# A single-core attention and MLP kernel, with and without TensorE's waits on its own finished work

## The chip, the core and the metric

The kernel runs on one core of a Trainium2 chip. A core has a matrix engine (TensorE, in the profile PE for its matmuls and PEld for its weight loads), a vector engine (VectorE, DVE), a scalar engine (ScalarE, ACT), a general engine (GpSimd, POOL) and a sync engine (SyncE, SP), which here only issues transfers. Each engine works through an instruction list of its own, and the lists meet only at semaphores: an instruction may wait until a semaphore has reached a count, and may raise one when it is done. The metric is the time of one execution on the device in microseconds (us).

## The reference

The computation has two parts, both in bfloat16. Part A is an attention layer with a memory that is carried from segment to segment. The 2048 tokens (512 wide) are normalised and cut into 64 segments of 32. For each segment, 8 memory rows are put ahead of the 32 tokens, and 32 heads of width 128 attend over the 40 rows. The first 8 rows of the output become the next segment's memory, so the 64 segments form a chain. Part B is an MLP (512 to 1792 to 512, with gelu) behind two layer norms.

```python
for s in range(n_seg):
    h = jnp.concatenate([mem, x[:, s*32:(s+1)*32, :]], axis=1)
    q, k, v = (jnp.einsum('btd,dhe->bhte', h, W) for W in (Wq, Wk, Wv))
    scores = jnp.where(mask, jnp.einsum('bhqe,bhke->bhqk', q, k) * scale, -1e9)
    o = jnp.einsum('bhqk,bhke->bhqe', _softmax(scores), v)
    o = jnp.einsum('bhte,hed->btd', o, Wo)
    mem = o[:, :8, :]
    outs.append(o[:, 8:, :])
h = x + concatenate(outs)
h2 = h + MLP(layernorm(layernorm(h)))
```

## The kernel before

Every operation is first recorded as an `Op` in a planner (`Sched`), with what it reads and writes and an expected duration. For TensorE one `Op` is a unit: a short fixed group of weight loads and matmuls, such as the four weight loads and four matmuls that make one 128-row step of a projection (`passes`, lines 931 to 952; its matmuls have line 946, its weight loads 944 and 946, and the matmuls that keep the weights of the unit before have line 689). Other units are the scores of the critical 8 rows (SC, line 1122), the full scores (SA, line 1179), the products with V (PV0, PV1 and PVA, lines 1153, 1157, 1225 and 1231) and the output projection (WO, line 1264, 8 units of 16 instructions; wo_B at line 1303 for a block of four segments).

The order of the units on TensorE is written out by hand (`ORDERS`): for each segment Q, K, V, the critical scores, filler work of the next block (F), the products, WO, SA. For the other engines `schedule` places each operation by planned times. `wire` then turns the dependencies into semaphore waits. Within TensorE no waits are needed, since its units run in order; `wire` gives it waits on ACT, DVE, POOL and on transfers alone.

Three further steps treat TensorE's instruction list as pieces of 256 instructions (`FETCH_N`), counted from `FETCH_AT`:

- `pads` (from line 497) adds up to 8 weight loads to a unit, which repeat a load that could have been left out. These shift where the borders between pieces fall. It chooses them by a cost over the planned time between two borders and over a lateness that depends on the unit in which the border falls (`LATE`).
- `windows` (from line 395) gives SyncE's transfers planned times between the borders.
- `pauses` (from line 374) looks at every unit that is the first to start behind a border (`heads`, set in `align`). Among the units that start within the next `PAUSE_IN` = 64 instructions, it takes the first `PAUSES` = 3 that wait for nothing, and makes each wait until TensorE's own last unit that was planned to end `PAUSE_US` = 0.5 us before it has ended. That earlier unit then raises TensorE's semaphore if it did not do so already.

`pauses` is the last step of `finalize`, behind the second `wire`. `emit` calls `align` once more behind it; there a unit's length in instructions counts half of its waits rounded down, so one wait adds nothing. The instruction list holds 156 heads, and `pauses` adds 407 waits: 116 in WO units, 147 in Q and K units, 71 in V units, 52 in F units and 21 outside the segments. It adds 156 semaphore increments, which makes 1266 on TensorE in all.

Of the kernel before, what the change touches and what calls it, by code (L numbers as in the profile page):

```python
# [27 lines left out]
LATE = dict(Q0=0.1, K0=0.1, Q1=-0.5, K1=-0.4, V0=2.0, SC0=2.0, SC1=1.6, V1=1.8, F=1.3, PV0=1.0, PVA=1.0, PV1=0.95, WO=0.4, F2=0.5, SA=0.5)  # L28
KEEP = True
WINDOWS, WIN_LO, WIN_HI, WIN_BEHIND = True, 1.0, -0.8, 0.4  # L30
PAUSES, PAUSE_IN, PAUSE_US = 3, 64, 0.5
KEPT, LEAD = 3, 9
REST = (0, 1, 4, 5, 6, 8, 9)
ORDER0 = (6, 7, 8, 9, 10, 11, 0, 1, 2, 3, 4, 5, 12, 13)
# [1746 lines left out]
```

## Time and profile before

| | |
|---|---|
| median of 3 runs | 804.04 us (802.3 to 804.13) |
| the profiled execution, whole | 805.6 us |
| its span, first to last instruction | 803.9 us |
| mean granted TensorE clock | 0.996 |
| TensorE matmuls busy | 770.4 us (96%) |
| VectorE, ScalarE, GpSimd busy | 73%, 66%, 39% |

The span holds an opening of some 52 us in which weights arrive, 63 segments of about 10.3 us up to about 700 us, and the MLP. The profile names each group of instructions by source line, engine, operation and the tiles it writes and reads, gives the idle time of the engine ahead of it, and what ended that idle time. "issue" as the ender means that the profile shows nothing that the engine waited for. Idle times under 0.15 us are not listed.

### The profile page before, as it was taken

The page shows a single profiled execution, that of the slowest core. Times are in us where ns is not written, and L with a number is a line of the kernel's source. Part 1 is how long each engine was busy: PE and PEld are TensorE (multiplying, and loading weights), DVE is VectorE, ACT ScalarE, POOL GpSimd, SP SyncE. Part 2 cuts the span into 40 slices and gives each one's busy share as a digit, 9 for nine tenths or more (in the row PEclk, how much of TensorE's full clock was granted, in tenths as well). Part 3 has the DMA queues.
Part 4 walks back from the last instruction along what each step waited for, and adds up shares of the span by engine and source line. Part 5 has one row for each costly group of instructions (what it writes and reads, how often), then busy time and mean ns, then how long its engine had stood idle before and what let it go on. Part 6 is the DMA issues. An engine that isn't in the chain of part 4 may idle for free.

```text
span 803.9 us, 44855 instructions
## 1 busy us (share of the span) xinstructions
PE 770.4 (96%) x19573; PEld 423.6 (53%) x20093; DVE 585.3 (73%) x1865; ACT 529.2 (66%) x1381; POOL 311.4 (39%) x836
## 2 busy tenths in 40 slices
PE   4788999999999999999999999999999999999998
PEld 1345455555555555556665555556556564544443
DVE  3267888888888888888888888888888887833111
ACT  1446777767776777776767777777776777653342
POOL 3013223444343444444434444444453425276200
PEclk9989999999999999999999999999999999999999
DMA  8960000111201010103020201030112222266200
GB/s 337 393 194 11 3 21 20 24 38 23 37 15 46 10 50 10 44 11 57 4 52 8 52 9 50 11 50 4 50 31 62 45 58 53 62 184 157 53 27 26
DMA packets 65453, 48.11 MB, mean 60 GB/s; under 512 B 29028, under 2 KB 61676, under 8 KB 65260
## 3 DMA queue, kind: packets, MB, share of 16 engines
q1 hardware_dynamic: 64928, 44.98, 20.4%
q8 instruction: 156, 2.56, 1.4%
q14 instruction: 37, 0.30, 0.1%
q10 hardware_dynamic: 332, 0.27, 0.1%
HBM read 31.08 MB, written 8.13 MB: 49 GB/s over the span
## 4 chain that ended last, share of the span: by engine, by line
PE 91%; DMA 2%; DVE 2%; SPq 2%; issue 1%; ACT 1%; DVEq 0%
PE high L946 33%; PE high L689 17%; PE quad L1264 15%; PE quad L1667 6%; PE high L1660 5%; PE high L1303 3%; DMA WQ<-in_A_Wq_dram 2%; SPq L849 2%; PE quad L1122 2%; PE quad L1179 2%; PE quad L1225 2%; PE high L1459 2%; PE high L1153 1%; PE quad L1153 1%; PE high L1264 1%
## 5 line engine op out<-in xcount | busy, mean ns | idle before, releaser
L946 PE MATMUL high<-WQ,hT 128*32 128x512 bf16 x1796 | 158.2, 383 | 3.8 <-DVE hT L1270 3.0
L1202 POOL TENSOR_TENSOR PA<-SA,rsa 128x256 bf16<-128x256 f32 x64 | 39.6, 619 | 235.5 <-DVE rsa L1194 148.0
L689 PE MATMUL high<-WK,hT 128*32 128x512 bf16 x1260 | 127.3, 379 | 0.1
L1264 PE MATMUL quad<-WO,OT 128*32 128x256 bf16 x4032 | 122.7, 273 | 0.2 <-issue 0.2
L946 PE MATMUL high<-WV,hT 128*32 128x512 bf16 x1528 | 117.0, 381 | 0.0
L965 ACT ACTIVATE kq<-high 128x512 bf16<-128x512 f32 x160 | 94.2, 598 | 26.7 <-PE high L946 23.3
L964 ACT CAST kq<-high 128x512 bf16<-128x512 f32 x161 | 93.7, 582 | 21.4 <-PE high L946 19.6
L1264 PEld LDWEIGHTS quad<-WO,OT 128*32 128x32 bf16 x4032 | 101.9, 97 | 6.9 <-issue 1.7
L1210 POOL COPY BD<-PTA 32x128 f32<-32x128 f32 x256 | 79.6, 311 | 16.3 <-DVE PTA L1206 0.6
L946 PEld LDWEIGHTS high<-WQ,hT 128*32 128x32 bf16 x1796 | 52.8, 95 | 62.0 <-issue 28.9
L987 DVE STREAM_TRANSPOSE KALL<-kq 128x256 f32<-128x256 f32 x160 | 69.4, 434 | 10.9 <-ACT kq L964 8.1
L964 ACT CAST VS<-high 128x512 bf16<-128x512 f32 x126 | 73.1, 580 | 0.0
L944 PEld LDWEIGHTS <-hT 128*32 128x32 bf16 x3064 | 50.7, 96 | 32.7 <-DVE hT L1270 6.3
L1276 DVE STREAM_TRANSPOSE TT<-quad 128x256 f32<-128x256 f32 x63 | 28.3, 449 | 50.8 <-PE quad L1264 50.7
L1663 ACT ACTIVATE WQ<-high,b1t 128x512 bf16<-128x512 f32 x42 | 28.9, 687 | 51.9 <-PE high L1660 51.9
L964 ACT CAST OT<-quad 128x128 bf16<-128x128 f32 (+1 forms) x128 | 47.8, 375 | 21.8 <-PE quad L1157 21.5
L1021 ACT COPY KALL<-KALL 128x128 f32<-128x128 f32 x62 | 18.5, 298 | 59.0 <-PE quad L1179 58.8
L987 DVE STREAM_TRANSPOSE QT<-kq 128x256 f32<-128x256 f32 x128 | 54.8, 428 | 1.9 <-ACT kq L965 1.6
L946 PE MATMUL high<-WK,hT 128*32 128x512 bf16 x788 | 55.4, 379 | 0.0
L1122 PEld LDWEIGHTS quad<-KALL,ZC 128*32 128x32 bf16 x2016 | 32.3, 96 | 42.2 <-POOL BD L1210 18.1
L689 PE MATMUL high<-WV,hT 128*32 128x512 bf16 x520 | 54.5, 387 | 0.0
L1316 POOL TENSOR_TENSOR opT<-TTB,TTS 32x64 bf16<-32x64 f32 x128 | 40.0, 312 | 35.0 <-DVE opT L1270 18.6
(182 smaller groups left out, 1612.4 us busy)
## 6 DMA issues: line engine op xcount, KB each, us to landing
WV<-in_A_Wv_dram SPq DMA_DIRECT2D x4, 1024.0 KB, 10.5
WK<-in_A_Wk_dram SPq DMA_DIRECT2D x4, 1024.0 KB, 18.5
WQ<-in_A_Wq_dram SPq DMA_DIRECT2D x4, 1024.0 KB, 20.4
WO<-in_A_Wo_dram SPq DMA_DIRECT2D x16, 256.0 KB, 7.6
v_last<-VSB SPq DMA_DIRECT2D x60, 64.0 KB, 2.2
VBD<-v_last SPq DMA_DIRECT2D x60, 64.0 KB, 2.6
h_mid<-xr SPq DMA_DIRECT2D x16, 128.0 KB, 2.0
WQ<-h_mid SPq DMA_DIRECT2D x4, 512.0 KB, 4.2
```

Of the source, the lines that this page charges most:

```text
L689: return e.add_instruction(mybir.InstMatmult(name="I-%d" % (4000000 + _kept[0]), engine=mybir.EngineType.PE, start_tensor_calc=start, stop ...
L944: e.ldweights(l, tile_position=(0, 32 * j))
L946: ins = e.matmul(o, l, m, start=(k == 0), stop=(k == DC - 1), tile_position=(0, 32 * j), skip_group_check=True)
L964: return {"act": (lambda e: e.copy(out, src), t_act(n, ps_)), "dve": (lambda e: e.tensor_copy(out, src), 0.155 + 1.0e-3 * n * fast)}
L965: return {"act": (lambda e: e.mul(out, src, scale_), t_act(n, ps_)), "dve": (lambda e: e.tensor_scalar(out, src, scale_, None, ALU.mult), ...
L987: S.op("dve", lambda e: e.transpose(out, src), reads=[("kq", i)], writes=[key], dur=t_dve(256) + 0.02)
L1122: ins = e.matmul(o[32 * j:32 * j + 32, :], zc_window(h), rhs, start=False, stop=(i == 3), tile_position=(0, 32 * j), skip_group_check=True)
L1210: S.narrow(S.op("pool", lambda e, j=j, rows=rows: e.tensor_copy(words(BD[rows, par, :, j, :, :]), words(PTA[rows, 0:4])), reads=["PTA"], w ...
L1264: ins = e.matmul(ps[bank][32 * j:32 * j + 32, 0:256], lhs(slot(h)), wo_cols(h, b), start=(k == 0), stop=(k == 15), tile_position=(0, 32 * ...
L1316: return e.tensor_tensor(o[32 * q:32 * q + 32, c:c + 2], x, y, ALU.add)
L1660: ins = e.matmul(ps[bank][:, 0:SBT], W1[:, cc, fc * P:(fc + 1) * P], hnT_of(k)[:, cc, :], start=(cc == 0), stop=(cc == DC - 1))
L1667: S.op("pe", lambda e: e.matmul(quad[:, t, :], gT_of(k, fc)[:, t * P:(t + 1) * P], W2[:, fc, :], start=(fc == (0 if k else ORDER0[0])), st ...
```

## The change

One constant changes, and with it `pauses` adds no wait and no increment. The waits on other engines and on transfers stay.

```diff
-PAUSES, PAUSE_IN, PAUSE_US = 3, 64, 0.5
+PAUSES, PAUSE_IN, PAUSE_US = 0, 64, 0.5
```

The loop that reads it:

```python
for first in self.heads:
    n, i = 0, first
    while n < PAUSES and i < len(pe) and pe[i].at < pe[first].at + PAUSE_IN:
        o = pe[i]
        j = bisect.bisect_right(ends, o.start - PAUSE_US) - 1
        if not o.waits and 0 <= j < i:
            o.waits = [pe[j]]
            pe[j].sig = True
            n += 1
        i += 1
```

## The prediction

> **What bounds the kernel now.** I read the page first, its busy shares and its chain, and then asked the trace for the idle time of TensorE alone.
>
> ```profile
> span 803.9 us, 44855 instructions
> PE 770.4 (96%) x19573; PEld 423.6 (53%) x20093; DVE 585.3 (73%) x1865; ACT 529.2 (66%) x1381; POOL 311.4 (39%) x836
> PE 91%; DMA 2%; DVE 2%; SPq 2%; issue 1%; ACT 1%; DVEq 0%
> ```
>
> TensorE's matmuls (PE) are busy for 96% of the span and make 91% of the chain that ended last. The weight loads (PEld) run beside them at 53%. A change that only touches TensorE's stream can win what idle time that stream has, or add to it. The next view splits the span: each row gives the stretch, its length, and then the busy time of PE, PEld, DVE, ACT and POOL.
>
> ```profile
> 0.00:52.00 52.00, 31.98 (x481) 13.63 (x465) 17.05 (x41) 17.53 (x40) 7.07 (x30) 0.93 0.96 348
> 52.00:93.00 41.00, 36.59 (x1100) 21.21 (x1132) 31.52 (x104) 26.10 (x73) 13.46 (x38) 1.00 0.10 18
> 93.00:350.00 257.00, 255.00 (x7401) 145.07 (x7564) 217.11 (x708) 188.61 (x513) 107.22 (x299) 1.00 0.12 27
> 350.00:660.00 310.00, 308.16 (x8916) 178.15 (x9352) 262.89 (x860) 227.08 (x619) 133.81 (x369) 1.00 0.16 35
> 660.00:702.00 42.00, 39.89 (x1140) 21.64 (x1032) 33.89 (x108) 29.15 (x77) 17.00 (x46) 1.00 0.23 60
> 702.00:803.90 101.90, 98.79 (x564) 43.95 (x552) 22.89 (x48) 40.74 (x61) 32.88 (x54) 1.00 0.34 88
> ```
>
> The opening (20.0 us idle) waits for weights to arrive, which the change does not touch. In the steady middle, 93 to 660 us, PE is idle for 257.00 - 255.00 + 310.00 - 308.16 = 3.8 us. What is that idle time? The waits of the matmul stream from 70 to 660 us (total us, times, longest):
>
> ```profile
> PE quad L1179 <- issue: 2.1, 8, 0.4
> PE high L946 <- DVE hT L1270: 1.5, 2, 0.8
> PE high L946 <- issue: 0.7, 3, 0.4
> PE high L1153 <- DVE PTC L1139: 0.5, 1, 0.5
> PE high L1157 <- issue: 0.3, 2, 0.2
> PE quad L1264 <- issue: 0.2, 1, 0.2
> ```
>
> Fourteen of these sixteen waits (8 + 3 + 2 + 1) are "issue": TensorE waits for nothing that the profile can name. They sum to 2.1 + 0.7 + 0.3 + 0.2 = 3.3 us. Two of them in order of time:
>
> ```profile
> 307.96 0.21 PE L1179 MATMUL quad<-KALL,QT 128*32 128x40 bf16 x5
> 308.48 0.35 PE L1179 MATMUL quad<-KALL,QT 128*32 128x40 bf16 x27 [0.31 <-issue]
> ...
> 616.93 0.39 PE L946 MATMUL high<-WQ,hT 128*32 128x512 bf16 x3
> 617.67 0.39 PE L946 MATMUL high<-WQ,hT 128*32 128x512 bf16 x1 [0.35 <-issue]
> ```
>
> The break falls inside one group of equal matmuls: after 5 of the 32 of L1179, after 3 of the 4 of L946. No tile can be missing there, since the group's operands were complete before its first matmul. What is missing is the next instruction. The profile shows that instructions come in pieces:
>
> ```profile
> q8 instruction: 156, 2.56, 1.4%
> ```
>
> 2.56 MB in 156 transfers is 16.4 KB each, and 1.4% of 16 engines' 803.9 us over 156 is an estimated 1.15 us per transfer. Between 93 and 350 us there are 7401 + 7564 matmuls and weight loads, which is 58 pieces of 256 in 257 us, or 4.4 us a piece. So each piece has to be requested, brought (1.15 us) and taken up within about 4.4 us, and at 14 of the some 132 borders between 70 and 660 us (by the same 4.4 us, an estimate) it came late. [...]
>
> **The change, part by part.** With PAUSES at 0 the loop in `pauses` adds nothing. Walking the program's own instruction list, I count 156 heads (first unit behind a border), 407 waits of TensorE on its own semaphore, and 156 semaphore increments that exist for these alone (of 1266). All 407 waits and 156 increments go. Nothing moves: the order on every engine, the padding weight loads, the borders and the DMA windows are all fixed before or without these waits, and a single wait rides in the weight load that has it, so no instruction is saved.
>
> *The waits themselves, against the path.* A wait costs time if TensorE runs dry at it. The matmul rows above name no release by PE. The weight-load port does:
>
> ```profile
> PEld high L946 <- PE high L946: 9.5, 28, 0.5
> PEld L944 <- PE high L946: 3.0, 7, 0.7
> PEld L944 <- PE high L689: 0.4, 1, 0.4
> PEld quad L1264 <- PE high L1157: 0.2, 1, 0.2
> ```
>
> At 28 + 7 + 1 + 1 = 37 places an own-work wait was the last thing that a weight load waited for; the port stood idle 9.5 + 3.0 + 0.4 + 0.2 = 13.1 us before them, 0.35 us each. Matmuls already issued cover that idle time: PE shows no gap there. Direct gain: 0 at one end; at the other, all 3.8 us of idle time of the middle, if "issue" hid them. I take 0, because the breaks above fall inside groups, where no such wait stands (a wait stands at a unit's first instruction). If the cover were gone the waits would cost up to 13.1 us now, and removing them would win it; nothing in the rows says that it is gone.
>
> *The increments.* 156 increments fewer on matmuls that run anyway: 0, from both sides, since no engine but TensorE reads these values.
>
> *The side effect on the fetch.* The 407 waits all stand in the first 64 instructions behind a border, so right behind the point at which one piece is used up and the next has to be asked for. While the front of TensorE's stream is held, it cannot run on through the new piece. Whether a hold brings the request forward, or holds it up, no row shows; this is the unknown of the forecast. I bound it. Its size per place is the hold itself, 0.35 us. Its number lies between 0 and 37 places (holds that were the last release). So the slip of the fetch sums to between 0 and 37 x 0.35 = 13 us, in the one direction or the other. A slip costs only where the piece is already just in time. That share lies between 14 of 132 borders (0.1, those which stall now) and all. I take a quarter, nearer the low end because that is the end with a row. And I take the direction "later without the waits": the stream then runs on, with the units behind the border already to be sent, before the next stop gives room, and the next stop is another engine's wait or a full stream. Cost: 37 x 0.35 x 0.25 = 3.2 us, between 1.3 (a tenth) and 13.
>
> *Where a later fetch hits.* TensorE stalls a little more at L1179 and at the first units of L946, as now. Vector, Scalar and GpSimd then wait for PE and shift with it: DVE at 73% and ACT at 66% have room, so nothing else becomes late first.
>
> *Sum.* 0 (waits) + 0 (increments) + 3.2 (fetch) = +3.2 us. The profiled execution took 805.6 us for its span of 803.9; on that basis the changed kernel takes 808.8. The median of the runs shown is 804.04, 1.6 us below the profiled one, and the forecast is for such a median: 804.04 + 3.2 = 807.2 us.
>
> [...]
>
> **The rivals.**
>
> *Nothing happens.* The request is made when the border is crossed, whatever stands behind it. All 407 waits stand behind it, so none can delay or hasten it. For it: 370 of the 407 are not seen to be the last release of anything. Against it: the 37 that are. Time: 804.0 us. [...]
>
> *Faster.* The waits sit at the front of the stream just behind the border, and what is held there delays the taking up of the piece, so that the following border is reached with less in hand. Without them TensorE arrives with more work already issued and the 14 breaks shrink. Price: the breaks' 3.3 us, and as the profile counts PE as busy to the modelled end of a matmul (379 ns in the row below, against a start every 0.22 us in the timeline), some 0.16 us more at each: 3.3 + 14 x 0.16 = 5.5 us if all go, half of it if half do.
>
> ```profile
> L689 PE MATMUL high<-WK,hT 128*32 128x512 bf16 x1260 | 127.3, 379 | 0.1
> ...
> 616.71 0.40 PE L689 MATMUL high<-WK,hT 128*32 128x512 bf16 x4
> ```
>
> Half gives 801.3 us, all 798.5. It decides from half of the breaks on (2.8 us is over what can be told). Against it: the holds are covered and long over when the next border comes 4.4 us later.
>
> *Much slower.* Each of the 37 holds is what makes the request early, and every border is just in time: 13 us, 817 us. For it: TensorE has 3.8 us of idle time in 567, so a delay has nowhere to go. Against it: 118 of 132 borders show no stall, so most have some slack.
>
> *That the change does not do what it says* can only mean that waits of other kinds remain: of the units behind borders many wait for ACT, DVE or POOL anyway. Those hold the front too and weaken the effect; this belongs to "nothing happens".
>
> **How the numbers follow.** A measurement of this kernel can tell about 0.3%, 2.4 us: the runs shown lie between 802.3 and 804.13. Chances: a slower fetch as forecast, 0.50 (its own range 805 to 813); nothing, 0.32; faster, 0.12; much slower, 0.06. Slower by over 0.3% (above 806.5) needs 2.4 us: I give that 0.40 of the first case's 0.50, and the last case's 0.06, so 0.46. Within 0.3%: 0.32, 0.10 of the first and 0.03 of the faster case, 0.45. Faster: 0.09. The range goes from 801.5 (most of the faster case at half price) to 814 (short of the extreme).
>
> **What would show it.** Right: the "issue" rows of the matmul stream grow from 14 events and 3.3 us in 70 to 660 us to some 20 to 25 events and 5 to 6 us, with breaks inside groups; the middle's PE idle time grows from 3.8 to about 7 us; the weight-load rows released by PE vanish; the instruction queue still shows 156 transfers. If idle "issue" stays at 3.3 us and the time too, the waits had no hold on the fetch. If "issue" falls, the direction was wrong. The prediction fails outright if the loss appears at another place than at borders, such as in waits for DVE or ACT.

## The result, and the profile after

The changed kernel takes 822.75 us (median of four, 818.5 to 824.5) against 803.76 us of the kernel before (median of four with one execution more than ahead of the prediction, 802.3 to 804.13): a ratio of 1.0234, interval 1.0211 to 1.0258. It is slower, as forecast, but by 19 us where the forecast was 3.2 us and its range ended at 814 us.

The profiled execution of the changed kernel took 818.5 us and lies 4.2 us below its median; the one before took 805.6 us, 1.6 us above its median. The two traces therefore differ by 818.5 - 805.6 = 12.9 us, and the sums below are made against that. The page of the changed kernel, its span, busy shares, chain, instruction queue and its output projection (matmul count, busy time and mean ns, idle time ahead):

```profile
span 816.8 us, 44855 instructions
...
PE 771.5 (94%) x19573; PEld 423.3 (52%) x20093; DVE 586.1 (72%) x1865; ACT 529.7 (65%) x1381; POOL 310.9 (38%) x836
...
q8 instruction: 156, 2.56, 1.3%
...
PE 90%; issue 2%; DMA 2%; DVE 2%; SPq 2%; ACT 1%; DVEq 0%
...
L1264 PE MATMUL quad<-WO,OT 128*32 128x256 bf16 x4032 | 125.9, 273 | 13.1 <-issue 13.1
```

The L1264 row on the page of before:

```profile
L1264 PE MATMUL quad<-WO,OT 128*32 128x256 bf16 x4032 | 122.7, 273 | 0.2 <-issue 0.2
```

The same work is done in the same pieces: counts and transfers are those of before, and the order of the instructions is the same on every engine. What grew is "issue", and on one line: L1264, the output projection WO, now stands idle for 13.1 us where it stood for 0.2 us.

The stretches of the steady middle (columns as in the prediction), here 93 to 672 us since the segments end later:

```profile
93.00:358.00 265.00, 259.20 (x7496) 144.90 (x7644) 220.20 (x720) 191.82 (x522) 108.81 (x305) 1.00 0.11 26
358.00:672.00 314.00, 305.12 (x8803) 177.83 (x9268) 258.88 (x845) 223.01 (x609) 131.74 (x364) 1.00 0.15 34
```

PE is idle for 5.8 + 8.9 = 14.7 us of it, against 3.8 us before. The clock column says 1.00 in both, as before. The waits of the matmul stream from 70 to 672 us (total us, times, longest) say at what:

```profile
PE quad L1264 <- issue: 11.7, 16, 1.3
PE high L946 <- DVE hT L1270: 1.5, 2, 0.8
PE quad L1179 <- issue: 1.3, 4, 0.3
PE high L1153 <- DVE PTC L1139: 0.5, 1, 0.5
PE high L1303 <- issue: 0.4, 1, 0.4
PE high L1157 <- issue: 0.2, 1, 0.2
PE high L946 <- issue: 0.2, 1, 0.2
```

The two waits for VectorE are unchanged to the tenth. "Issue" went from 14 events and 3.3 us to 23 events and 11.7 + 1.3 + 0.4 + 0.2 + 0.2 = 13.8 us, and 16 of the 23 are at WO. One of them in the timeline:

```profile
453.79 0.50 PE L1264 MATMUL quad<-WO,OT 128*32 128x256 bf16 x9
455.11 1.71 PE L1264 MATMUL quad<-WO,OT 128*32 128x256 bf16 x55 [0.82 <-issue]
456.55 0.70 PE L1303 MATMUL high<-WO,OTB 128*32 128x512 bf16 x8
```

A group of 64 equal matmuls is broken after 9, and the other 55 come 0.82 us late. The reading is again that the next instruction piece is missing, and the place fits it: counted out in the program's own instruction list, in pieces of 256, the late matmul is the first, the second or the fourth instruction behind a border at all 14 "issue" stops of before and at all 23 of now.

Listed idle time grew by 13.8 - 3.3 = 10.5 us, and the profile counts the modelled end of each matmul as busy. What the stops cost is better seen by setting each unit's first matmul in one trace beside the same one in the other. Segments 5 to 60 take 14.6 us more than before, and 14.8 us more in their WO units alone; the other units come to -0.2 us. Segment 5, on the other hand, starts at 91.1 us and before at 92.9 us, so the trace of the changed kernel had a shorter opening. 14.6 - 1.8 = 12.8 us is the difference of the traces to within 0.1 us.

### The profile page after: what moved, and what is told of

The parts are those of the page before. It is cut to its first block, busy times and chain, and to the rows that moved or that the text cites. A ratio compares the mean times of both kernels' runs of the same rounds, so it can differ in the third digit from the quotient of the medians.

```text
span 816.8 us, 44855 instructions
## 1 busy us (share of the span) xinstructions
PE 771.5 (94%) x19573; PEld 423.3 (52%) x20093; DVE 586.1 (72%) x1865; ACT 529.7 (65%) x1381; POOL 310.9 (38%) x836
## 4 chain that ended last, share of the span: by engine, by line
PE 90%; issue 2%; DMA 2%; DVE 2%; SPq 2%; ACT 1%; DVEq 0%
PE high L946 32%; PE high L689 17%; PE quad L1264 15%; PE quad L1667 6%; PE high L1660 5%; PE high L1303 3%; DMA WQ<-in_A_Wq_dram 2%; PE quad L1179 2%; PE quad L1122 2%; SPq L849 2%; PE quad L1225 2%; PE high L1459 2%; PE high L1153 1%; PE quad L1153 1%; PE high L1264 1%
## 5 line engine op out<-in xcount | busy, mean ns | idle before, releaser
L946 PE MATMUL high<-WQ,hT 128*32 128x512 bf16 x1796 | 157.6, 380 | 3.4 <-DVE hT L1270 3.0
L1264 PE MATMUL quad<-WO,OT 128*32 128x256 bf16 x4032 | 125.9, 273 | 13.1 <-issue 13.1
L946 PE MATMUL high<-WV,hT 128*32 128x512 bf16 x1528 | 116.5, 380 | 0.0
L1264 PEld LDWEIGHTS quad<-WO,OT 128*32 128x32 bf16 x4032 | 102.0, 97 | 22.5 <-issue 17.9
L946 PEld LDWEIGHTS high<-WQ,hT 128*32 128x32 bf16 x1796 | 52.4, 95 | 61.1 <-issue 28.9
L987 DVE STREAM_TRANSPOSE KALL<-kq 128x256 f32<-128x256 f32 x160 | 69.5, 434 | 11.7 <-ACT kq L964 8.4
L946 PE MATMUL high<-WK,hT 128*32 128x512 bf16 x788 | 55.4, 379 | 0.0
```

The lines of the kernel that those rows point to most:

```text
L946: ins = e.matmul(o, l, m, start=(k == 0), stop=(k == DC - 1), tile_position=(0, 32 * j), skip_group_check=True)
L987: S.op("dve", lambda e: e.transpose(out, src), reads=[("kq", i)], writes=[key], dur=t_dve(256) + 0.02)
L1264: ins = e.matmul(ps[bank][32 * j:32 * j + 32, 0:256], lhs(slot(h)), wo_cols(h, b), start=(k == 0), stop=(k == 15), tile_position=(0, 32 * ...
```

## Where the late pieces come from

The page does not date single instruction transfers, but the trace records them, and the semaphore counts date TensorE's units. From both I worked out how long behind the crossing of a border the next transfer starts, by the first unit behind the border. What the trace dates is the start of a transfer, not what asks for it; "the request" stands below for that start. (A border between two pieces is crossed when the first instruction behind it runs. It is dated here from the last unit ahead that raised the semaphore, with the planned time from there. V0 and V1 are the two halves of a segment's V projection, K1 the second half of K, SC0 and SC1 the two halves of the critical scores, F the filler work.)

| first unit behind the border | borders | median lateness before | after |
|---|---|---|---|
| V0 | 20 | 0.99 us | 2.16 us |
| K1 | 6 | 0.65 us | 1.88 us |
| F | 36 | 0.85 us | 0.91 us |
| PV1 | 6 | 0.78 us | 0.79 us |
| K0 | 14 | 0.69 us | 0.65 us |
| WO, the next behind one in V0 or K1 | 26 | 0.72 us | 1.63 us |
| WO, others | 8 | 0.59 us | 0.73 us |

The 27 borders ahead of Q0, Q1 and SA units are left out; dated by the start of the first instruction behind the border, their medians moved by less than 0.1 us. The request slips behind borders in V0 and K1, by 1.2 us. The 0.9 us at the WO borders that follow them is the stop itself: a crossing is dated from a unit ahead of it, so a stop at the crossing counts as lateness. Dated by the start of the first instruction, their medians are 1.00 us before and 1.08 us after, and those of V0 1.36 and 2.40 us.

By this second dating the next border behind V0 is 4.1 us away (median, before), and at the 16 stops at WO the first matmul behind the border ran 2.15 to 2.76 us (median 2.4 us) after the transfer of its piece had started. Before, by an estimate with the same 2.4 us, 1.36 + 2.4 = 3.8 us fits into 4.1 us; after, 2.40 + 2.4 = 4.8 us misses by 0.7 us, about the mean length of these stops (11.7 / 16 = 0.73 us). The piece that misses is the one whose border lies 256 instructions behind V0, and that is in WO.

In the changed kernel 14 of the 22 transfers behind these borders from 70 to 672 us start 1.00 to 1.11 us behind VectorE's release of SC1; six start earlier and two later. SC1 is a unit with two waits, on GpSimd and on VectorE. In the traces of the two kernels no weight load and no matmul has more than one wait (1124 weight loads have one before, 720 after); for SC1's second there is a semaphore instruction of its own, ahead of the weight load, and it is that one that carries the wait on VectorE. TensorE has 388 semaphore instructions in either trace. In the kernel before, the same transfers mostly start 1.2 to 1.4 us behind VectorE's release of SC0, the first half of the same scores, although SC1 has its separate semaphore instruction there too.

## The experiments

The expectations name the theories by letters. What they say of the way of the request is supposed; the runs show times, stops and the starts of transfers. **A**: only the holds behind borders in V0 and K1 matter, because they stop the stream and the request gets out in the stop. **B**: the loss belongs to all borders, in proportion to the waits. **C**: the presence of the waits is enough, whether they hold anything or not. **D**: without the holds the request is kept back until the front of the stream has got past SC1's separate semaphore instruction. **E**: the request is late only because no stop, of whatever form, comes ahead of SC1's own wait. **F**: the opposite of D, that any separate semaphore instruction lets a request out. In the kernels with more lines, WO has another line number.

**Waits only behind V0 and K1** (e1; 78 of the 407).

```diff
 for first in self.heads:
+    if pe[first].tag is None or pe[first].tag[1] not in ("V0", "K1"):
+        continue
```

> Keeps the waits behind the 26 borders whose first unit is a V0 or K1 unit (78 of the 407 waits) and drops the other 329. Theory A: without the waits the request for the next piece goes out some 1 us later, but only behind these borders, since behind them TensorE runs on through the V units without a stop until the second critical scores (SC1); at all other borders another stop stands near. Expected by A: all of the loss is won back, 803 to 805 us, the issue row of L1264 at 0 to 0.5 us. Rival B: each wait brings its own border's request forward a little, so the gain is in proportion to the waits kept, 78/407 of 19 us: about 819 us.

**Waits everywhere else** (e2; the other 329): the same test reversed.

> The mirror: the 329 waits behind all other borders are kept, the 78 behind V0 and K1 borders are dropped. Theory A: 820 to 824 us, the issue row of L1264 at some 11 to 13 us in 15 to 17 events, as without any waits. Rival B: about 808 us.

The first took 804.29 us (1.001, interval 0.9993 to 1.0026), the second 821.56 us (1.023, 1.0209 to 1.025). Their waits at WO, the first's:

```profile
PE quad L1266 <- issue: 0.5, 2, 0.3
```

and the second's:

```profile
PE quad L1266 <- issue: 11.8, 16, 1.2
```

So 78 waits behind 27 borders (26 in the table, and one ahead of 70 us) hold the whole effect and the other 329 do nothing that can be measured. B falls. In e1's trace no row of the weight loads names PE as the releaser, though the whole effect is there; in e2's 31 places do, and there is no effect.

**The waits on older work** (e3). Each of the 407 stays, but on a unit that ended 3 us ahead, so that it should hold up nothing: in the trace that unit had ended 2.58 us or more before the waiting load ran, against a median of 0.25 us in the kernel before.

```diff
-PAUSES, PAUSE_IN, PAUSE_US = 3, 64, 0.5
+PAUSES, PAUSE_IN, PAUSE_US = 3, 64, 3.0
```

> All 407 waits stay in number and nearly in place, but each waits for a unit that was planned to end 3.0 us before instead of 0.5 us, so that it is as good as always satisfied when it is reached. Theory A (what counts is that the front of the stream is held): no effect of the waits, 818 to 824 us. Rival C (what counts is that a weight load carries a wait at all, whether it holds or not): 803 to 805 us.

It took 822.32 us (1.0227, 1.0195 to 1.0259), the time of the kernel without waits:

```profile
PE quad L1264 <- issue: 13.0, 16, 1.2
```

C falls: the number of waits is that of the kernel before, and what differs is how long ahead they were released. **One wait in place of three** (e4, `PAUSES` 1) and **0.8 us in place of 0.5** (e7, `PAUSE_US`) ask how much hold is needed.

> One wait behind each border instead of three (148 waits), the first that finds room. Theory A: one hold behind a V0 border (the first free unit behind the first critical scores) lasts only some 0.1 to 0.2 us; if one stop is enough for the request the time is 803 to 806 us, if it takes a stop of some length it lies between, 808 to 816 us. Rival B (in proportion): 816 us.

> Three waits behind each border, each for work planned to end 0.8 us before instead of 0.5, so that the holds are some 0.3 us shorter. Theory A: a dose in between, some of the V0 borders late and some not: 808 to 818 us. If 0.8 us is still inside TensorE's lead: 803 to 805 us; if the hold is gone: 819 to 823 us.

With one wait 816.8 us (1.0182, 1.0139 to 1.0226), which is also what B forecast, but e1 and e2 exclude B; with three waits at 0.8 us 821.09 us (1.0215, 1.0176 to 1.0254). The waits at WO with one wait:

```profile
PE quad L1264 <- issue: 9.4, 13, 1.0
```

and with 0.8 us:

```profile
PE quad L1264 <- issue: 12.4, 15, 1.1
```

With one wait the lateness behind V0 falls into two groups, at 0.9 and at 2.15 us; a border is either helped or not. At 0.8 us about as many are in the second group as without any waits: with 0.3 us more of planned age the waits win back next to nothing (1.0215 against 1.0234). No wait of that kernel was released less than 0.41 us before its load ran; behind V0 and K1 in the kernel before it was 0.06 to 0.42 us.

**SC1 without its separate semaphore instruction** (e5). No waits on finished work. One of SC1's two waits goes to the V1 unit ahead, and one more weight load takes the place of the semaphore instruction (62 units), so that no border moves.

```diff
-PAUSES, PAUSE_IN, PAUSE_US = 3, 64, 0.5
+PAUSES, PAUSE_IN, PAUSE_US = 0, 64, 0.5
...
+        for was, o in zip(pe, pe[1:]):
+            if o.tag is not None and o.tag[0] > 1 and o.tag[1] == "SC1" and len(o.waits) == 2 and not was.waits:
+                was.waits, o.waits = o.waits[:1], o.waits[1:]
+                o.ni, o.more[0] = o.ni + 1, True
...
+                if more[0]:
+                    e.ldweights(zc_window(16 * r), tile_position=(0, 0))
```

> None of the 407 waits, but the second critical scores (SC1) lose their separate semaphore instruction: of its two waits (GpSimd, VectorE) the first moves onto the V1 unit just ahead, where it rides in a weight load, and one more weight load takes the place of the instruction that goes, so that all 156 borders stay where they are (62 units changed). Theory D: without the own-work waits TensorE's instruction front reaches SC1's separate semaphore instruction too early and sits in it until VectorE is done, and the request for the next piece cannot leave before; without that instruction it leaves as with the waits: 803 to 808 us. Rival E: what delays the request is only that no stop comes before SC1's own wait, of whatever form: 819 to 824 us.

**A separate semaphore instruction more** (e6), on waits long satisfied, on the V0 unit behind SC0 at the 26 borders in V0 and K1; a padding weight load less keeps the borders.

```diff
...
+                if o.tag is not None and o.tag[1] == "V0" and not o.waits and pe[i - 1].tag[1] == "SC0":
+                    self.longer.append((o, [pe[bisect.bisect_right(ends, o.start - t) - 1] for t in (3.4, 3.0)]))
...
```

> None of the 407 waits, but behind 26 borders (V0, K1) the V unit just behind the first critical scores gets two waits on own work that ended 3 us and more before: as good as always satisfied, yet with a separate semaphore instruction; one padding weight load fewer behind it keeps the borders. Rival F: the request leaves when the next separate semaphore instruction is executed, whatever it waits for: 803 to 808 us. Theory D and E: no effect, 819 to 824 us.

Without the separate instruction: 802.59 us (0.9984, 0.9967 to 1.0001), lateness behind V0 0.95 us. With one more: 820.9 us (1.021, 1.0185 to 1.0234). The first one's waits name no "issue" at WO at all:

```profile
PE quad L1188 <- issue: 1.3, 4, 0.4
...
PE high L950 <- issue: 0.7, 2, 0.4
```

and the second one's:

```profile
PE quad L1282 <- issue: 12.2, 14, 1.2
```

F falls, and the stops are gone without any wait on finished work, as D has it. But the wait that went to V1 is itself a hold ahead of SC1. Two kernels take these apart.

**The hold on V1 alone** (e9). V1 gets the wait, and SC1 keeps both of its own and its separate instruction. Against e5's edit:

```diff
-                was.waits, o.waits = o.waits[:1], o.waits[1:]
-                o.ni, o.more[0] = o.ni + 1, True
+                was.waits = o.waits[:1]
```

> No waits on finished work. The first of SC1's two waits is also put on the V1 unit ahead of it (as in e5), but SC1 keeps both of its waits, and so its separate semaphore instruction. If the separate instruction as such is what holds the request up (theory D), the request still slips: about 820 us, with ten or more 'issue' stops at the WO matmuls. If what helped in e5 was the new hold on V1, which stands ahead of SC1 and lets the request out there, the time stays at about 803 us and the WO row has at most 4 stops. By D in its weaker form (the separate instruction harms only while TensorE has to stand in it) the hold on V1 takes the standing away, so about 803 us too: a slow result would speak for D alone, a fast one for the hold or the weaker form.

It took 820.19 us (1.0214, 1.0196 to 1.0232). Its matmul stream:

```profile
PE quad L1272 <- issue: 12.0, 17, 1.1
```

Its weight loads name GpSimd at V1 (line 949), and SC1 still stood for VectorE (line 1129):

```profile
PEld quad L1129 <- DVE KALL L990: 15.0, 40, 0.7
PEld high L949 <- POOL ZC L1013: 14.5, 46, 0.5
```

The first row alone does not show a hold, since the port stands idle ahead of V1 without the wait too (17.1 us in segments 5 to 60 of the changed kernel, 17.6 us here). The dates point to one: behind V0 and K1, GpSimd's release came 0.04 to 0.25 us before the load of V1 ran, as near as the releases that help in the kernel before. This wait ahead of SC1 does not help. The weaker form of D is not excluded by it, since SC1 still stood for VectorE.

**The form alone** (e13). Both waits stay at SC1, in place; one more weight load carries GpSimd's, the weight load behind it VectorE's, and there is no separate semaphore instruction (62 units). Nothing is held earlier. The order of the two waits turns round, since the separate instruction had VectorE's and stood first.

```diff
+            if o.tag is not None and o.tag[0] > 1 and o.tag[1] in FORM and len(o.waits) == 2 and not any(w.is_dma for w in o.waits):
+                o.waits = sorted(o.waits, key=lambda w: w.eng == "dve")
+                o.more[0] = True
...
```

> No waits on finished work; nothing is moved. SC1's two waits stay at SC1 and in the same place, but the separate semaphore instruction that carries one of them is replaced by one more weight load that carries it (62 units). If it is the form of the waiting instruction that holds the request up (theory D), the slip goes: 801 to 804 us and at most 4 'issue' stops at the WO matmuls, as in e5, with no hold added ahead of SC1. If the hold that e5 put on V1 is needed as well, it stays at about 820 us with ten or more stops.

It took 801.87 us (0.9989, 0.9968 to 1.0011), with these stops:

```profile
PE quad L1200 <- issue: 0.9, 3, 0.4
PE high L955 <- issue: 0.7, 3, 0.3
PE quad L1285 <- issue: 0.6, 2, 0.4
```

One and the same pair of waits at one and the same place cost some 20 us when one of them was in a semaphore instruction of its own (822.75 us), and nothing that can be measured when it was in a weight load (801.87 us). The order is not what counts: e5 and e9 both have GpSimd's wait ahead, on V1, and differ in the form of VectorE's wait as these two do. E falls, since nothing was put ahead of SC1 here. It is the form of the wait at SC1 that the slip went with in this kernel: by the median the next transfer started 2.16 us behind a border in V0 in the changed kernel and 0.91 us in e13. Why, no run shows.

**The first remedy once more (e10), and both remedies together (e11).**

> The kernel of e5 once more, in more rounds: 802.6 us, ratio 0.998, if e5's gain of 1.6 us was real; 804 us, ratio 1.000, if it was chance.

> e5's edit together with the waits on finished work as in the kernel before. If both only let the request out behind V0 and K1, the second adds nothing: 802 to 804 us, the WO row with at most 4 stops. If the waits also do something at the other borders, it comes out below e5, at 801 us or less. If they cost something of their own, above it, at 804 to 805 us.

e5's kernel again took 800.37 us (0.9972, 0.9958 to 0.9986), and with the 407 waits put back beside its edit 799.89 us (0.9969, 0.9957 to 0.9981). The gain of the first remedy was real, and both times lie below what was expected. The change of this case, 19 us here before, is worth 0.5 us once SC1 has no separate semaphore instruction, which is within what can be told.

**The same at other units.** First e5's edit at PV0 too (e12, 47 units more):

> No waits on finished work; e5's edit extended to PV0, so that 47 more units with two waits lose their separate semaphore instruction, each for one more weight load. If the separate instructions also delay the requests behind the F borders, the remaining 'issue' stops at the score matmuls (L1179 of the kernel before, 2.1 us) shrink and the time is 800 to 802 us. If they matter only behind V0 and K1, it is e5's time, 802 to 804 us, or a little more for the 47 weight loads.

It took 799.12 us (0.9959, 0.9945 to 0.9974), which is not clear of e10's 0.9972, but the stops at the scores are gone; all rows of its matmul stream:

```profile
PE high L950 <- DVE hT L1284: 1.5, 2, 0.8
PE high L1166 <- DVE PTC L1148: 1.0, 2, 0.5
PE high L950 <- issue: 0.5, 1, 0.5
PE quad L1166 <- DVE PTC L1148: 0.2, 1, 0.2
```

Then the form alone (e14) at SC0, SC1, PV0 and PV1 (`FORM = ("SC0", "SC1", "PV0", "PV1")`, 233 weight loads for 233 semaphore instructions):

> e13's edit at SC0, SC1, PV0 and PV1, wherever such a unit has two waits and none on a transfer. If separate semaphore instructions hold up the requests behind the other borders too, the 'issue' stops at the score matmuls go as in e12, and the time is 798 to 801 us. If only the place of e12's holds did that, it is e13's time, 801 to 804 us.

It took 793.67 us (793.12 to 795.7), 0.9869 of the kernel before (0.9849 to 0.9889), 10 us below the kernel before and below what was expected. Its waits and its middle:

```profile
PE high L955 <- DVE hT L1291: 1.5, 2, 0.8
PE high L1173 <- DVE PTC L1154: 1.1, 3, 0.4
PE quad L1173 <- DVE PTC L1154: 0.2, 1, 0.2
```

```profile
93.00:350.00 257.00, 256.92 (x7504) 144.79 (x7735) 220.43 (x722) 192.64 (x524) 109.96 (x303) 1.00 0.14 27
350.00:650.00 300.00, 299.84 (x8814) 176.71 (x9385) 257.22 (x847) 223.40 (x610) 133.25 (x366) 1.00 0.17 36
```

No "issue" stop is left, PE's idle time in the middle is 0.08 + 0.16 = 0.24 us, and the lateness behind V0 is -0.31 us: the next transfer starts ahead of the border. That would fit a slip at SC0's separate instruction as well, but four kinds of units changed at once, and no run takes them apart. Set beside the trace of before, unit by unit, segments 5 to 60 take 10.05 us less: 7.1 us in units that hold a border, and 2.9 us in units that hold none. In the second part the step from PVA's first matmul to PV1's gains 0.06 to 0.15 us in each of the 50 segments that have no border there, 3.9 us in all, and other steps give some of it back. In e12, which leaves PV1 as it was, these 50 steps differ by 0.05 us in all from before. So these 3.9 us, about 0.08 us a segment, went with the separate instruction at PV1, without any late piece.

**The planner told of the lateness** (e8). One kernel keeps the waits and gives the planner the lateness that the trace of before has (`LATE` of V0, V1, SC0 and SC1 at 1.3, of F at 1.1, `FETCH_IN` 1.4), which moves eight borders into V1 and others elsewhere.

> The kernel before, its 3 waits at 0.5 us kept, but the padding is laid out anew for what the traces show with the waits: lateness 1.3 us behind V0, V1, SC0 and SC1 borders instead of 1.6 to 2.0, 1.1 behind F instead of 1.3, and 0.3 us more for a piece to be taken up (1.4 instead of 1.1). Theory A: the 14 breaks that are left shrink by a half or more, 799 to 803 us. Rival: the lateness of other borders takes over, 803 to 810 us.

It took 809.16 us (1.0066, 1.0041 to 1.009), where theory A had 799 to 803 us. It is inconclusive for the cause, since it moves paddings as well.

## Why the prediction was wrong

- **What bounds the kernel.** Right. TensorE without a reserve (3.8 us idle in the 567 us of the middle before), some 132 borders, stops that are late instruction pieces: the new loss is of this kind. (The prediction's rows have 17 waits and not sixteen; 14 of them are "issue", as it says.)
- **The waits and the increments themselves at nothing.** Right. 329 of the 407 went without a measurable difference.
- **The direction.** Right, though half by its reason. Behind V0 and K1 14 of 22 transfers start 1.00 to 1.11 us behind another engine's release (VectorE's, at SC1), as the reason had it. But it said nothing of the form of that wait, and by the form the time goes: 822.75 us, and 820.19 in e9, with VectorE's wait in the separate semaphore instruction, 801.87 with it in a weight load (e13). That a stop as such gives room for the request, or that the stream can be full, no run shows.
- **The size: the step that failed.** In "37 x 0.35 x 0.25 = 3.2 us" the places and the length are both taken from rows that have nothing to do with the effect. None of the 37 places stands behind a border in V0 or K1, where e1 finds the whole effect. And the idle time there is not the waits': in the changed kernel the port for weight loads stands idle at 36 of the same 37 units, for 13.7 us where it was 13.1, and the profile now says "issue". "L946 <- issue" was 61.5 us in 184 places before; after:

```profile
PEld high L946 <- issue: 69.6, 209, 0.5
...
PEld L944 <- issue: 3.7, 9, 0.6
```

What the runs show in its place is a slip of 1.2 us behind 26 borders: the next transfers mostly start 1.00 to 1.11 us behind VectorE's release of SC1, and before 1.2 to 1.4 us behind that of SC0. No length of a hold is in it. The true product in the traces is 16 stops at WO of 0.73 us listed idle time, or 14.8 us in WO units. In the medians it is 19 us. No trace was taken of this kernel at that median; e3's, at 823.12 us, has 16.7 us more than before in segments 5 to 60, and where the rest lies is not shown.
- **The share.** "A quarter, nearer the low end because that is the end with a row" counted borders that stall now. What decides is the reserve of a border against a slip of 1.2 us, and that differs by place: from V0, 0.3 us. Of the 26 borders in V0 and K1, 17 led to a stop up to 672 us; the other 6 of the 23 stops stand elsewhere, and behind the other borders the transfers started at most 0.14 us later than before (the WO borders behind V0 or K1 apart).
- **The place.** Wrong. L1179 and L946 were named; their "issue" fell from 2.8 to 1.5 us. The new stops are at L1264. The count forecast, 20 to 25 events, came out at 23, but with 13.8 us and not 5 to 6, and that is luck: the forecast spread a small slip over all borders, where a large one falls on a few. The kernel's own table of latenesses (`LATE`) has V0 at 2.0 us and WO at 0.4; without the waits V0's is 2.16 us. The prediction did not use it as a list of places with the least reserve.
- **The rivals.** "Much slower" at 817 us is nearest in time, but by another mechanism ("every border is just in time"): by e1 all borders but 27 can do without the waits. "Nothing happens" rested on the request being made when the border is crossed, whatever stands behind it; the table of latenesses contradicts it (0.99 us behind V0 with the waits, 2.16 us without). "Faster" fell: the removal alone shrank no stop but some at L1179 and L946. The stops that it priced went in e12 and e14, which also take separate semaphore instructions away.

## What to carry to other kernels

Where TensorE has as little reserve as here (3.8 us idle in 567), give each border between instruction pieces a budget: lateness of the next transfer, time until the piece can be used, against the time to the next border. Here that was 2.40 + 2.4 us against 4.1 us behind V0, and the stops at WO had 0.73 us each. A slip of 1.2 us is then priced by the borders whose reserve is smaller (17 of 26 led to a stop), and not by the length of the waits that were edited. A releaser that the profile names is not yet a hold: look whether the same idle time stands there when the wait is gone (13.1 us at 37 places before, 13.7 us at 36 of them after). A TensorE unit that waits for two engines shortly behind a border is the place to look at first: here, letting an extra weight load carry one of the waits at SC1 took the stops at WO from 11.7 us to 0.6 us (e13), and at four kinds of units it made the kernel 1.3% faster than before (e14), without any wait on own work.

## What the runs showed that was not expected

- The transfer of the next instruction piece does not start at a fixed time behind the border. In the changed kernel 14 of 22 started 1.00 to 1.11 us behind VectorE's release of the separate semaphore instruction at SC1, and the median was 2.16 us behind a border in V0; with the same wait in a weight load it was 0.91 us (e13).
- Up to three own-work waits behind a border in V0 or K1, released 0.06 to 0.42 us before their loads ran in the kernel before, were enough for 804.29 us, without any idle time of the port that the profile puts down to them (e1). A wait on V1, next to SC1, released 0.04 to 0.25 us before its load ran, was not (e9, 820.19 us), nor were waits released 2.58 us before and more (e3, 822.32 us). What a hold needs for it, in length or in place, stays open.
- 233 weight loads more in place of as many semaphore instructions made the kernel 10 us shorter than the one before the change, though the port for weight loads was busy for 53% in either.
